# The Nyquist column of a folded DFT: from the matmul to a VectorE add at the eviction

## The chip, the cores and the metric

The kernel runs on one core of a Trainium2 chip. Time is the device time of one execution in microseconds; a kernel's time is the median over several executions. One execution is also recorded by the hardware profiler, and all durations of single instructions come from that one.

The engines are called PE (TensorE: matmul; PEld is its weight load), DVE (VectorE), ACT (ScalarE), POOL (GpSimd) and SP (SyncE, which only issues DMAs here).

## What is computed

The input x has 8 batches of 3008 tokens and 256 features (fp32). The reference, cut to what matters:

```
X = fft(x, axis=1); X = fft(X, axis=2); x = X.real        # over the tokens, then over the features
xt = x.transpose(0, 2, 1)
h  = max(xt @ w_tok1, 0) @ w_tok2                         # token mixing: 3008 -> 256 -> 3008
u  = x + h.transpose(0, 2, 1)
out = u + max(u @ w_ch1, 0) @ w_ch2                       # channel mixing: 256 -> 1536 -> 256
```

Only the real part is wanted, so the kernel uses the symmetry of the DFT: features d and 256 - d are added (even part) and subtracted (odd part) first, and cosines act on the even part and sines on the odd part. The even part has 129 values: d = 0, 1 to 127, and the Nyquist value d = 128, whose cosine over the output index is +1, -1, +1, and so on.

## The kernel before

All matmuls are in fp16 with sums in fp32. Every batch goes through two halves.

The *front* of a batch, `front(b)`, is a generator; each `yield` ends a step, and the main loop takes steps one by one.

- `fold` (GpSimd, for batch 0 VectorE) makes the even and odd parts `eo`: in its 256 features, columns 0 to 128 are the even part and 129 to 255 the odd part.
- 8 steps of the first token stage: matmuls of `eo` into PSUM tile pz, copied to `z`. The first half of `z` has features 0 to 127 of `eo`, the second half features 128 to 255; so partition 0 of the second half is the Nyquist value and partitions 1 to 127 are the odd part.
- 12 steps of the d stage, which the change touches (lines 439 to 446). Step g multiplies the two halves of z, as weights (128x128), by two tables: `td1` (259 columns) and `td0` (131 columns), both into PSUM tile pw. The result `w` has columns 0 to 130 for the cosine sums (column 1 and 130 are two half sums) and columns 132 to 258 for the sine sums. The odd part gives columns 132 to 258 only; of the 259 columns of `td1` the first 132 are zero except in row 0, which holds +0.5 and -0.5: there the Nyquist value is added to the cosine columns. `copy` (lines 287 to 291) evicts pw into w: with 0 on ScalarE, with 1 on VectorE. VectorE takes every second step of batch 0, and ScalarE all others.
- 2 steps with `pt` (line 455, 12 matmuls of 130 and 12 of 127 columns each), 3 steps with `pq` and `py` (line 482), and 12 steps with `pu` (line 506) finish the token mixing and give `ut`, the transposed u.

Every PSUM tile of the front comes from one pool with three buffers (tag "f": pz, pw, pt, px, py, pq, pu). `ps_mm` has three more for pc, and `ps_out` two for po.

The *channel half* of a batch works on 6 chunks of 512 tokens, each in 4 subtiles. In a subtile the program order is: `mm1`, three groups of two matmuls of 512 columns into pc (line 539), evicted with the max on ScalarE (line 542) twice and on VectorE (line 87 through `ts`) once; `mm2` for the chunk before, 12 matmuls of 256 columns into po (line 560), whose sums VectorE adds (line 574) in every second subtile; and then some steps of the next batch's front.

Nothing is reordered: each engine runs its instructions in program order, and the number of steps in every subtile is written out by hand:

```
plan = [[0] * 11 + [3, 3, 2, 4, 4, 4, 1, 1, 2, 1, 4, 4, 4],
        [2] * 4 + [2] * 6 + [1, 1] + [1] * 3 + [1, 2] * 4 + [0]]
```

The first list holds while batch 0 is in its channel half, the second after that. So the 12 d steps of batch 0 run alone, in setup; those of batch 1 run in three subtiles of batch 0, four in each (in the first and third behind a step of batch 0 with pu); and those of batches 2 to 7 run in six subtiles each, two in each, 72 steps in all.

Of the kernel before, what the change touches and what calls it, by code (L numbers as in the profile page):

```python
# [9 lines left out]
FP16 = mybir.dt.float16  # L10
FP32 = mybir.dt.float32
I32 = mybir.dt.int32
AT = mybir.AluOpType
# [6 lines left out]
P = 128  # L20
# [14 lines left out]
WD = 259  # L35
TWO23 = float(2.0 ** 23)
PI2 = float(2 * np.pi)
# [3 lines left out]
def kernel(  # L41
# [9 lines left out]
    nc = tc.nc  # L51
# [8 lines left out]
    const = ctx.enter_context(tc.tile_pool(name="const", bufs=1))  # L60
# [11 lines left out]
    def ps_f(name, dt=FP32, n=512):  # L72
        return psum.tile([P, n], dt, tag="f", name=name, bufs=3)
# [11 lines left out]
    def ts(out_, in_, s1, op0, s2=None, op1=None, eng=nc.vector):  # L85
        if op1 is None:
            eng.tensor_scalar(out=out_, in0=in_, scalar1=s1, scalar2=None, op0=op0)  # L87
        else:
            eng.tensor_scalar(out=out_, in0=in_, scalar1=s1, scalar2=s2,
                              op0=op0, op1=op1)  # L90
# [7 lines left out]
                                   in1=pcol[:], op0=AT.mult, op1=AT.add)  # L98
# [7 lines left out]
                                   op0=AT.mult, op1=AT.add)  # L106
# [53 lines left out]
    for t in (tp, tq):  # L160
        for i in range(2):
            h = slice(64 * i, 64 * i + 64)
            nc.scalar.activation(
                out=t[h, :, 64 - 64 * i:128 - 64 * i],
# [15 lines left out]
                                   op0=AT.mult, op1=AT.add)  # L180
# [6 lines left out]
                                   op0=AT.mult, op1=AT.add)  # L187
    nc.vector.scalar_tensor_tensor(out=reff[:], in0=eq32[:], scalar=1472.0, in1=reff[:],
                                   op0=AT.mult, op1=AT.add)
# [3 lines left out]
                                   op0=AT.mult, op1=AT.add)  # L193
    nc.vector.scalar_tensor_tensor(out=offq[:], in0=mid[:], scalar=-752.0, in1=tmp[:],
                                   op0=AT.mult, op1=AT.add)
# [27 lines left out]
    def reduced(m, period, nrow, width, eng=nc.vector):  # L223

        v = gen.tile([P, width], FP32, tag="gv", bufs=2, name="gv")[0:nrow, :]
        eng.tensor_scalar(out=v, in0=m, scalar1=1.0 / period, scalar2=TWO23,
                          op0=AT.mult, op1=AT.add)
        eng.tensor_scalar(out=v, in0=v, scalar1=-TWO23, scalar2=-float(period),
                          op0=AT.add, op1=AT.mult)
        r = gen.tile([P, width], FP32, tag="gr", bufs=2, name="gr")[0:nrow, :]  # L230
        eng.tensor_tensor(out=r, in0=v, in1=m, op=AT.add)
        return r

    def sin(out_, in_, scale):
        nc.scalar.activation(out=out_, in_=in_, func=AFT.Sin, scale=scale)
# [51 lines left out]
    def copy(e, out_, in_):  # L287
        if e:
            (nc.vector, nc.gpsimd)[e - 1].tensor_copy(out=out_, in_=in_)
        else:  # L290
            nc.scalar.activation(out=out_, in_=in_, func=AFT.Copy)  # L291
# [8 lines left out]
    pl = nc.gpsimd  # L300
# [28 lines left out]
    ts(md[:, 128:255], jrow[:, 1:128], pcol[:], AT.mult, eng=pl)  # L329
    rd = reduced(md[:], 256, P, 255, pl)  # L330
    td0 = const.tile([P, 131], FP16, tag="td0")
    td1 = const.tile([P, WD], FP16, tag="td1")
    sin(td0[:, 2:130], rd[:, 0:128], PI2 / 256)
    sin(td1[:, 132:WD], rd[:, 128:255], PI2 / 256)
    pl.memset(td0[:, 0:1], 1.0)
    ts(td0[:, 1:2], td0[:, 129:130], 0.5, AT.mult, 0.5, AT.add, eng=pl)
    ts(td0[:, 130:131], td0[:, 129:130], 0.5, AT.mult, -0.5, AT.add, eng=pl)
    ts(td0[0:1, :], td0[0:1, :], 0.5, AT.mult, eng=pl)
    pl.memset(td1[:, 0:132], 0.0)
    pl.memset(td1[0:1, 0:2], 0.5)  # L340
    pl.memset(td1[0:1, 3:130:2], 0.5)
    pl.memset(td1[0:1, 2:130:2], -0.5)


    tcol, sgn = pvec("tcol"), pvec("sgn")
# [29 lines left out]
    def w2_cols(b, c):  # L375
        return (w2p if b else w2v)[:, :, :, 8 * c:min(8 * c + 8, NQ)]
# [30 lines left out]
    def front(b):  # L407
# [3 lines left out]
        for t0 in (11, 6, 1):  # L411
            for half in range(2):
                c = slice(half * P, (half + 1) * P)
                pz = ps_f("pz")
                for k in range(5):
                    nc.tensor.matmul(pz[:, 96 * k:96 * k + 96], lhsT=eo[:, t0 + k, c],  # L416
                                     rhs=t1n[:].rearrange("p a b k -> p (a b k)"),
                                     start=True, stop=True)
# [4 lines left out]
        for half in range(2):  # L423
# [3 lines left out]
                             rhs=t1n[0:NQ, half, 0, :],  # L427
                             start=True, stop=True)
            if half:
                nc.tensor.matmul(pz[0:1, 0:24], lhsT=eo[0:NQ, 0, P:P + 1],  # L430
                                 rhs=t1n[0:NQ, 0, 0, :], start=True, stop=True)
            nc.tensor.matmul(pz[:, 24:96], lhsT=eo[:, 16, c],  # L432
                             rhs=t1b[:].rearrange("p a k -> p (a k)"),
                             start=True, stop=True)
# [3 lines left out]
        w = perb.tile([P, NG, WD], FP16, tag="w", name="w", bufs=2)  # L438
        for g in range(NG):
            pw = ps_f("pw")  # L440
            za = z[:, 0, 2 * g:2 * g + 2, :].rearrange("p a b -> p (a b)")
            zb = z[:, 1, 2 * g:2 * g + 2, :].rearrange("p a b -> p (a b)")
            nc.tensor.matmul(pw[:, 0:WD], lhsT=zb, rhs=td1[:], start=True, stop=False)  # L443
            nc.tensor.matmul(pw[:, 0:131], lhsT=za, rhs=td0[:], start=False, stop=True)  # L444
            copy(g % 2 and b == 0, w[:, g, :], pw[:, 0:WD])
            yield


# [1 line left out]
        for th in range(2):  # L450
            c = slice(th * P, (th + 1) * P)
            pt = ps_f("pt1")
            for o, n, f, hw in ((0, 130, 0, hp), (130, 127, 132, hq)):
                for g in range(NG):
                    nc.tensor.matmul(pt[:, o:o + n], lhsT=hw[:, g, c],  # L455
                                     rhs=w[:, g, f:f + n],
                                     start=(g == 0), stop=(g == NG - 1))
            if th == 0:
                px = ps_f("px")
                nc.tensor.matmul(px[:, 0:NG], lhsT=perm[:], rhs=w[:, :, 130],  # L460
                                 start=True, stop=True)
# [15 lines left out]
        for c in range(3):  # L477
            py, pq = ps_f("py"), ps_f("pq")
            for o, f, tab in ((pq, 131, tq), (py, 1, tp)):
                for k in range(4):  # L480
                    g = 4 * c + k
                    nc.tensor.matmul(o[:, P * k:P * k + P], lhsT=w[:, g, f:f + P],  # L482
                                     rhs=tab[:, g, :], start=True, stop=True)
            qs = perb.tile([P, CW], FP32, tag="qs", name="qs", bufs=2)
            nc.scalar.activation(out=qs[:], in_=pq[:], func=AFT.Copy)  # L485
            for h, op in ((0, AT.subtract), (1, AT.add)):
                nc.vector.tensor_tensor(out=yt[:, h, CW * c:CW * c + CW], in0=py[:],  # L487
                                        in1=qs[:], op=op)
# [10 lines left out]
        for c in range(NCH):  # L499
            f0 = CW * c  # L500
            n = min(CW, S - f0)
            for h in range(2):
                minus = c >= 3
                pu = ps_f("pu")
                for th in range(2):
                    nc.tensor.matmul(pu[:, 0:n], lhsT=uu[:, th, int(minus), h, :],  # L506
                                     rhs=w2_cols(b, c)[:, th],
                                     start=(th == 0), stop=(th == 1))
# [3 lines left out]
                else:  # L512
                    y = yt[:, h, f0:f0 + n]
                nc.vector.tensor_tensor(  # L514
                    out=ut[:, h, f0:f0 + n].rearrange("p (a b) -> p a b", b=64),
                    in0=pu[:, 0:n].rearrange("p (b a) -> p a b", b=64),
                    in1=y.rearrange("p (a b) -> p a b", b=64), op=AT.add)
# [85 lines left out]
    if BB > 1:  # L603
        x_tiles[1] = load_x(1)
    own = front(0)
    take(own, 4)
    carried(tts_p, hp)
# [16 lines left out]
    turned_u = {(0, 0): turn_u(0, 0)}  # L624
    for b in range(BB):
        nxt = front(b + 1) if b + 1 < BB else iter(())
        done, folded = 0, False
        for c in range(NCH):
# [60 lines left out]
```

## Time and profile before

| | |
|---|---|
| median of 9 runs | 644.05 us (642.79 to 644.88) |
| the profiled execution | 644.87 us, span 643.1 us |
| PE busy | 617.7 us (96%), 4778 matmuls |
| DVE, ACT, POOL busy | 331.3, 317.5, 251.1 us |
| granted TensorE clock, mean | 0.988 of full speed |
| line 443, pw, 128x259, 96 times | 274 ns each |
| line 444, pw, 128x131, 96 times | 221 ns each |
| line 291, ACT copy of pw to w, 90 times | 386 ns each |
| line 289, DVE copy of pw to w, 6 times | 426 ns each |

A line of the timeline or of the groups names the line of the program, the engine, the operation, the tiles (out<-in), their shapes and a count; a bracket holds how long the engine had been idle before and what ended that. A matmul's duration includes the time until its last result is out, and the next one starts long before that; the rate of matmuls is read from their starts. The chain of waits is followed back from the last instruction. In the table of stretches each row gives the stretch, its length, the busy time and count of PE, PEld, DVE, ACT and POOL, the granted clock, and the share of the DMA engines and their GB/s.

### The profile page before, as it was taken

What the parts mean: (1) busy time and instruction counts of PE and PEld (TensorE: products, weight loads), DVE (VectorE), ACT (ScalarE), POOL (GpSimd) and SP (SyncE); (2) the same over time, 40 slices, a digit from 0 to 9 for tenths busy, and PEclk for the clock granted to TensorE, in tenths of its full rate; (3) what the DMA queues carried; (4) which work ended last, traced back from release to release, by engine and by line L of the source; (5) the groups of instructions that cost most, each with busy time, mean ns of one, the idle gap of its engine ahead of it and who ended that gap; (6) DMA issues with size and microseconds to landing.
All of it is one profiled execution on the core that took longest, in us unless ns stands there. A gap on an engine that the chain in (4) does not pass through costs nothing.

```text
span 643.1 us, 11805 instructions
## 1 busy us (share of the span) xinstructions
PE 617.7 (96%) x4778; PEld 425.3 (66%) x4778; DVE 331.3 (52%) x702; ACT 317.5 (49%) x667; POOL 251.1 (39%) x250
## 2 busy tenths in 40 slices
PE   3789999999999999999999999999999999999996
PEld 3545667567766776667766676666766777666675
DVE  8755435733664437633565336643466336653442
ACT  7547465265535554365533655356533655334431
POOL 8819949669130880059411591039400000000000
PEclk9779999999999999999999999999999999999999
DMA  9992472732932268142763229223221521332332
GB/s 148 180 212 52 82 150 50 140 68 50 162 70 68 55 94 151 33 99 59 123 79 80 66 60 161 63 66 82 59 50 34 115 50 50 66 75 69 80 82 66
DMA packets 86550, 56.28 MB, mean 88 GB/s; under 512 B 54832, under 2 KB 83440, under 8 KB 85744
## 3 DMA queue, kind: packets, MB, share of 16 engines
q1 hardware_dynamic: 78240, 38.04, 27.7%
q0 software_dynamic: 8256, 17.49, 17.2%
q8 instruction: 37, 0.61, 0.4%
q14 instruction: 17, 0.14, 0.1%
HBM read 34.98 MB, written 24.64 MB: 93 GB/s over the span
## 4 chain that ended last, share of the span: by engine, by line
PE 93%; DMA 2%; DVE 2%; ACT 1%; POOL 1%; issue 1%; DVEq 0%; ACTq 0%; POOLq 0%
PE po L560 38%; PE pc L539 38%; PE pu L506 6%; PE pt L455 3%; DMA w1m<-in_moe_w_tok_dram 2%; PE pw L443 2%; PE pz L416 1%; PE pw L444 1%; PE py L482 1%; PE pq L482 1%; PE ph L365 1%; PE ph L363 1%; DVE yt L487 0%; DVE ut L514 0%; PE pz L432 0%
## 5 line engine op out<-in xcount | busy, mean ns | idle before, releaser
L542 ACT ACTIVATE c<-pc 128x512 f16<-128x512 f32 (+1 forms) x384 | 205.4, 588 | 171.8 <-PE pc L539 143.7
L560 PE MATMUL po<-wc,c 128*128 128x256 f16 x2256 | 276.4, 273 | 0.0
L560 PEld LDWEIGHTS <-c 128*128 128x128 f16 x2256 | 220.8, 98 | 63.1
L87 DVE TENSOR_SCALAR c<-pc 128x512 f16<-128x512 f32 (+1 forms) x192 | 130.5, 680 | 164.9 <-PE pc L539 145.9
L539 PE MATMUL pc<-ut,wc1p 128*128 128x512 f16 x576 | 141.3, 381 | 0.5 <-DVE ut L514 0.4
L539 PE MATMUL pc<-ut,wc1m 128*128 128x512 f16 (+1 forms) x576 | 134.9, 370 | 0.0
L574 DVE TENSOR_TENSOR osb<-po,rt 128x258 f32<-128x258 f32 (+3 forms) x240 | 74.7, 361 | 55.8 <-PE po L560 51.5
L539 PEld LDWEIGHTS <-wc1m 128*128 128x128 f16 x576 | 54.8, 98 | 54.0
L539 PEld LDWEIGHTS <-wc1p 128*128 128x128 f16 x576 | 53.1, 98 | 51.8 <-issue 5.6
L514 DVE TENSOR_TENSOR ut<-pu,yt 128x512 f16<-128x512 f32 (+1 forms) x96 | 61.6, 671 | 35.6 <-PE pu L506 35.6
L394 POOL TENSOR_TENSOR xd<-xp,xm 94x1024 f16<-94x1024 f16 x28 | 59.3, 2119 | 24.5 <-DVE c L87 13.8
L592 POOL COPY ch<-c 128x768 f16<-128x768 f16 x4 | 3.3, 824 | 155.6 <-DVE c L87 155.6
L395 POOL TENSOR_TENSOR xp<-xp,xm 94x1024 f16<-94x1024 f16 x28 | 59.4, 2120 | 2.2
L399 POOL TENSOR_TENSOR eo<-xp 94x512 f16<-94x512 f16 (+1 forms) x28 | 34.0, 1213 | 59.4 <-PE pz L432 58.2
L291 ACT ACTIVATE w<-pw 128x259 f16<-128x259 f32 x90 | 30.1, 386 | 49.6 <-PE pw L444 49.1
L594 POOL COPY c<-ch 128x768 f16<-128x768 f16 x4 | 3.3, 824 | 122.4 <-PE po L560 122.4
L291 ACT ACTIVATE z<-pz 128x480 f16<-128x480 f32 (+1 forms) x59 | 34.5, 674 | 24.4 <-PE pz L416 20.2
L506 PE MATMUL pu<-w2p,uu 128*128 128x512 f16 (+1 forms) x168 | 45.0, 379 | 1.2 <-DVE ut L514 1.2
L487 DVE TENSOR_TENSOR yt<-py,qs 128x512 f16<-128x512 f32 x48 | 30.7, 686 | 18.9 <-ACT qs L485 9.4
L403 POOL TENSOR_TENSOR eo<-xd 94x508 f16<-94x508 f16 (+1 forms) x28 | 33.7, 1204 | 0.0
L506 PEld LDWEIGHTS <-uu 128*128 128x128 f16 x192 | 19.0, 99 | 12.4 <-issue 3.4
L485 ACT ACTIVATE qs<-pq 128x512 f32<-128x512 f32 x24 | 14.1, 596 | 19.4 <-PE pq L482 9.2
(142 smaller groups left out, 378.8 us busy)
## 6 DMA issues: line engine op xcount, KB each, us to landing
out_dram<-osb SPq DMA_DIRECT2D x84, 256.0 KB, 3.4
xp<-in_x_dram POOLq DMA_DIRECT2D x16, 272.0 KB, 5.6
out_dram<-osb SPq DMA_DIRECT2D x12, 192.0 KB, 2.8
xp<-in_x_dram POOLq DMA_DIRECT2D x16, 127.5 KB, 5.9
rt<-ut SPq DMA_TRANSPOSE x96, 2.7
w2s<-in_moe_w_tok_dram POOLq DMA_DIRECT2D x1, 1504.0 KB, 19.0
w1p<-in_moe_w_tok_dram POOLq DMA_DIRECT2D x2, 384.0 KB, 10.3
wc<-in_moe_w_ch_dram POOLq DMA_DIRECT2D x1, 768.0 KB, 11.7
```

Source lines behind the costliest of these rows:

```text
L87: eng.tensor_scalar(out=out_, in0=in_, scalar1=s1, scalar2=None, op0=op0)
L291: nc.scalar.activation(out=out_, in_=in_, func=AFT.Copy)
L394: eng.tensor_tensor(out=xd[:, t, :], in0=xp[:, t, :], in1=rv, op=AT.subtract)
L395: eng.tensor_tensor(out=xp[:, t, :], in0=xp[:, t, :], in1=rv, op=AT.add)
L399: eng.tensor_tensor(out=eo[:, t, 1:129], in0=xp[:, t, 1:129], in1=xp[:, t, 255:127:-1], op=AT.add)
L403: eng.tensor_tensor(out=eo[:, t, 129:256], in0=xd[:, t, 1:128], in1=xd[:, t, 255:128:-1], op=AT.subtract)
L506: nc.tensor.matmul(pu[:, 0:n], lhsT=uu[:, th, int(minus), h, :], rhs=w2_cols(b, c)[:, th], start=(th == 0), stop=(th == 1))
L514: nc.vector.tensor_tensor(out=ut[:, h, f0:f0 + n].rearrange("p (a b) -> p a b", b=64), in0=pu[:, 0:n].rearrange("p (b a) -> p a b", b=64), ...
L539: nc.tensor.matmul(pc[:, 0:n], lhsT=wc[:, h, ct * P:(ct + 1) * P], rhs=ut[:, h, f0:f0 + n], start=(h == 0), stop=(h == 1))
L542: nc.scalar.activation(out=c1[:, ct, 0:n], in_=pc[:, 0:n], func=AFT.Relu)
L560: nc.tensor.matmul(po[0:n, o:o + D], lhsT=c1[:, ct, ks * P:ks * P + n], rhs=wc2[:, ct, :], start=(ct == 0), stop=(ct == NCT - 1))
L574: nc.vector.tensor_tensor(out=osb[r, ks_, j], in0=src[r, k0:k1, j], in1=rt[r, ks_, p], op=AT.add)
```

## The change

`td1` loses its first 131 columns: it has 128, of which the first is zero except for 0.5 in row 0, and its product with the second half of z is written to columns 131 to 258 of pw. Column 131 of pw then holds half of the Nyquist value, one number for each partition. The product with `td0` no longer adds onto it but is written to columns 0 to 130 by itself. At the eviction ScalarE copies the sine columns 132 to 258, in every step and batch, and VectorE writes columns 0 to 130 in one `scalar_tensor_tensor`: a new constant `alt` (+1, +1, -1, +1, ..., with 0 in the last column), times the number in column 131, plus the cosine columns. Column 131 of w is written later (from px), as before.

```diff
     td0 = const.tile([P, 131], FP16, tag="td0")
-    td1 = const.tile([P, WD], FP16, tag="td1")
+    td1 = const.tile([P, P], FP16, tag="td1")
+    alt = const.tile([P, 131], FP16, tag="alt")
     sin(td0[:, 2:130], rd[:, 0:128], PI2 / 256)
-    sin(td1[:, 132:WD], rd[:, 128:255], PI2 / 256)
+    sin(td1[:, 1:P], rd[:, 128:255], PI2 / 256)
...
-    pl.memset(td1[:, 0:132], 0.0)
-    pl.memset(td1[0:1, 0:2], 0.5)
-    pl.memset(td1[0:1, 3:130:2], 0.5)
-    pl.memset(td1[0:1, 2:130:2], -0.5)
+
+    pl.memset(td1[:, 0:1], 0.0)
+    pl.memset(td1[0:1, 0:1], 0.5)
+    pl.memset(alt[:], 1.0)
+    pl.memset(alt[:, 2:129:2], -1.0)
+    pl.memset(alt[:, 130:131], 0.0)
...
-            nc.tensor.matmul(pw[:, 0:WD], lhsT=zb, rhs=td1[:], start=True, stop=False)
-            nc.tensor.matmul(pw[:, 0:131], lhsT=za, rhs=td0[:], start=False, stop=True)
-            copy(g % 2 and b == 0, w[:, g, :], pw[:, 0:WD])
+            nc.tensor.matmul(pw[:, 131:WD], lhsT=zb, rhs=td1[:], start=True, stop=True)
+            nc.tensor.matmul(pw[:, 0:131], lhsT=za, rhs=td0[:], start=True, stop=True)
+            copy(0, w[:, g, 132:WD], pw[:, 132:WD])
+            nc.vector.scalar_tensor_tensor(
+                out=w[:, g, 0:131], in0=alt[:], scalar=pw[:, 131:132],
+                in1=pw[:, 0:131], op0=AT.mult, op1=AT.add)
             yield
```

In the changed kernel the two matmuls stand on lines 446 and 447 and the VectorE operation on line 449; later lines are shifted by six. Its line 291 is the ScalarE copy still.

## The prediction

> **What bounds the kernel now.** I read the page's busy times first, then the chain of work that ended last.
>
> ```profile
> PE 617.7 (96%) x4778; PEld 425.3 (66%) x4778; DVE 331.3 (52%) x702; ACT 317.5 (49%) x667; POOL 251.1 (39%) x250
> PE 93%; DMA 2%; DVE 2%; ACT 1%; POOL 1%; issue 1%; DVEq 0%; ACTq 0%; POOLq 0%
> ```
>
> TensorE is on 93% of the chain, so a moving column that is removed is worth its full time wherever TensorE runs without gaps. Whether it does where the changed lines stand, the timeline tells. There are three kinds of places: 12 of the 96 steps of the d stage belong to batch 0 and run alone in setup, 12 belong to batch 1 and run four at a time, and 72 (batches 2 to 7) run two at a time between the channel matmuls. First a pair of the 72:
>
> ```profile
> 141.44 0.27 PE L443 MATMUL pw<-td,z 128*128 128x259 f16 x1
> 141.55 0.22 PE L444 MATMUL pw<-td,z 128*128 128x131 f16 x1
> 141.60 0.27 PE L443 MATMUL pw<-td,z 128*128 128x259 f16 x1
> 141.64 0.76 DVE L574 TENSOR_TENSOR osb<-po,rt 128x258 f32<-128x258 f32 x2 [0.62 <-PE po L560]
> 141.72 0.22 PE L444 MATMUL pw<-td,z 128*128 128x131 f16 x1
> 141.77 1.46 PE L539 MATMUL pc<-ut,wc1p 128*128 128x512 f16 x6
> 141.81 0.66 ACT L291 ACTIVATE w<-pw 128x259 f16<-128x259 f32 x2 [1.26 <-PE pw L444]
> 143.27 0.69 DVE L87 TENSOR_SCALAR c<-pc 128x512 f16<-128x512 f32 x1 [0.88 <-PE pc L539]
> ```
>
> Starts, not durations, give the rate: 259 columns take 0.11 us, 131 take 0.055, a step takes 0.166, and the pc matmuls follow with no gap. The evictions lie beside them, and VectorE has 0.88 us idle before its next pc eviction. Between 138.39 and 153.00 us the stretch view gives PE 14.61 us busy of 14.61.
>
> In setup it is different:
>
> ```profile
> 31.45 0.69 DVE L289 CAST hq<-ph 128x512 f16<-128x512 f32 x1 [0.25 <-PE ph L365]
> 31.61 0.73 ACT L291 ACTIVATE w<-pw 128x259 f16<-128x259 f32 x2
> 32.06 1.30 DVE L289 CAST w<-pw 128x259 f16<-128x259 f32 x3
> ```
>
> The 12 steps of batch 0 run from 31.25 to 34.56, 0.276 us each although TensorE needs 0.166: they are paced by evictions into three PSUM buffers, with ScalarE and VectorE taking turns. Columns saved there are worth nothing by themselves.
>
> The last view is the waits:
>
> ```profile
> DVE uv L466 <- ACT sq L464: 24.9, 16, 2.5
> ```
>
> L466 reads only pt, not sq, and yet it waited 16 times of 16 for ScalarE's copy out of the same PSUM tile. Two engines that read one PSUM tile are put one after the other in this program. The changed eviction reads pw with both engines, and the instruction order of the changed kernel (which can be read before it runs) shows the same: each new VectorE operation waits for ScalarE's copy of its tile, and each later pw matmul that needs a buffer waits for VectorE. So the two halves of the eviction are a chain, not parallel.
>
> **TensorE, 72 steps.** 390 columns become 128 + 131 = 259. The nearest row for two such matmuls with alternating weights is the token stage, 130 and 127 columns, all 128x128 weights:
>
> ```profile
> 98.31 1.36 PE pt L455 x24
> ```
>
> 1.36 / 24 = 0.0567 us each, so a new step takes at most 0.113; scaling 0.166 by 259/390 gives 0.110. I take 0.112, a saving of 0.054 a step, 72 x 0.054 = 3.9 us (3.8 to 4.0). One thing has no row: the first matmul's output now begins at an odd PSUM column (131). Bounds: nothing, or at worst its 0.055 becomes 0.11, which takes the whole saving. I take nothing, as the token stage writes from mid-bank (column 130) and L443 and L444 have odd widths, all at the normal rate. No gain is possible beyond the columns.
>
> The Trainium skill speaks against this ("TensorE: Matmul & The Clock Gate", Back-to-back issue gap): it gives about 81 ns a matmul at 128 columns once weight loads are counted. By it, an estimate, a new step would take 0.162 us, 72 steps would save 0.3 us, and the whole sum would come to +0.7. The 0.0567 us above, with a weight load before every matmul, differs, and the measurement decides.
>
> **Eviction, the durations.** ScalarE's 128x259 copy (386 ns) becomes 128x127; the row is L464, 128x127 out of PSUM, 0.27 us, the next one about 0.20 later. VectorE gets 96 operations of 131 elements with one PSUM and one SBUF input; the row is L467, 128x127, 280 ns, with its successor starting 0.20 later (36.66, 36.86). Upper bound: two cycles for an element or a slow scalar, twice the 0.14 us by which 128x254 (416 ns) exceeds that row, so 0.42 us with a spacing of 0.34. It can't be under the 0.16 of the smallest rows. I take 0.28. VectorE rises by 96 x 0.28 - 6 x 0.43 = 24 us, ScalarE falls by 90 x 0.386 - 96 x 0.27 = 9 us.
>
> **Is that hidden in the 72 steps?** Behind the new operation in VectorE's queue is the pc eviction L87, for which the PSUM buffer of pc and then the po matmuls wait. In the pair above: osb ends at 142.40, the two new operations start at 142.32 and 142.52 (ScalarE is done by then) and end at 142.80, L87 is due at 143.27 less 0.11 of saved TensorE time, 143.16. A margin of 0.36; with the 0.42 us operation 0.08. Every second subtile has no osb and more room. Cost nothing; without that cover a pair would cost up to 0.5 us. The next pair's buffers are due at 144.2, 1.4 us after. The longest wait of osb for rt (0.6 us) fits too.
>
> **Batch 0, 12 steps.** VectorE starts at 32.06 as now, after hq. Then a buffer's round is: second matmul starts 0.055 after the first, result 0.22, to ScalarE 0.04, copy 0.27, to VectorE 0.03, operation 0.28, to TensorE 0.05: 0.945 us for three steps, 0.315 a step instead of 0.276. Rounds start on TensorE at 32.39, 33.34, 34.28; the last operation runs from 35.30 to 35.58, and the twelfth hp matmul, which reads it, starts at 35.63 instead of 34.56 + 11 x 0.057 = 35.19. Cost 0.44 us; with 0.42 us operations 1.3; if steps overlap better than this, 0.
>
> **Batch 1, 12 steps, four at a time.** The fourth step waits for the first one's buffer. In the first group VectorE is busy with ut until 87.49, its first new operation runs 87.41 to 87.69, the fourth step starts at 87.74 and pc at 87.85 (now 87.74): +0.11. In the second, osb holds VectorE until 91.31; the operation runs 91.25 to 91.53, the fourth step starts at 91.58, pc at 91.69 (now 91.32): +0.37. The third is like the first: +0.07. Sum +0.55, against 1.0 with the slow operation. So the 24 early steps lose 1.0 us together.
>
> **The rest.** GpSimd's four memsets of td1 (0.5 us at 24.3) become five of td1 and alt; what follows in its queue (perm at 25.94, the wc1 loads at 26.7) moves by 0.2 us at most, and perm is needed at 35.9, wc1 at 44.45. Sine widths are unchanged. Nothing.
>
> **Sum.** -3.9 + 0.44 + 0.55 = -2.9 us. The profiled execution took 644.87 us (span 643.1), at the top of the nine runs (642.79 to 644.88, median 644.05); the difference carries over to the median: 641.1 us, profiled about 642.0.
>
> **Rivals.**
> The clock falls. The granted clock halved at 40.4 us after a stretch of one 3.4 us grid step (steps of 3.41 fit the changes at 26.75, 40.37 and 47.15):
>
> ```profile
> 30.16:33.58 3.42, 3.26 (x29) 2.48 (x28) 2.70 (x7) 2.53 (x6) 2.81 (x6) 1.00 0.89 118
> 36.99:40.37 3.38, 1.58 (x25) 1.28 (x23) 0.97 (x5) 2.58 (x9) 0.00 (x0) 1.00 1.31 265
> 40.37:43.80 3.43, 2.97 (x15) 1.37 (x13) 3.43 (x8) 0.78 (x2) 0.00 (x0) 0.50 1.01 199
> ```
>
> A step with PE busy 47% led to half clock; after the change the step 30.16 to 33.58 has about 2.5 us busy of 3.42, 73%, where now it has 95%. No row says what 73% does. If the clock falls at 33.58, the token stage runs at half rate: +1.7 to 2.2 us, net -1.2 to -0.7, 642.9 to 643.4. The skill's same page (Part 1: The HAM clock gate) asks for at least one idle window of about 3.4 us before the clock drops. By it no drop comes here, and yet none would explain 40.4 either, where PE was 47% busy. Chance 0.08.
>
> The short matmul isn't short (the slower side). Each weight load of z lasts 98 ns. If L446 and L447 can't overlap theirs, a step takes 0.196 instead of 0.166: 72 x 0.03 = +2.2, with the early 1.0 +3.2 us, 647.3. It decides from 83 ns a matmul up. Against it stands 0.0567. The odd column at its worst belongs here too: no saving, +1.0 us, 645.0. Chance 0.07 together, most of it for the weight loads and their like.
>
> The hand-off is dearer: 0.42 us operations give -3.9 + 1.3 + 1.0 = -1.6, 642.4; still faster, part of the forecast's range. That the change doesn't do what it says is excluded by the instruction order: 96 VectorE operations, matmuls of 128 and 131 columns.
>
> **Numbers.** The forecast has 0.85, the clock 0.08, the long matmul 0.07. The range goes from -4.0 + 0.3 less 0.4 for the spread of medians, 639.9, to the far end of the clock case, 643.3. About 0.2% (1.3 us) is what can be told from no change, so faster means under 642.76: the forecast but for its upper tail, 0.83; the clock case and that tail are the same, 0.11; slower 0.06.
>
> **What would show it.** Right: L446 and L447 start 0.055 apart in the paired steps, the subtile of 2.94 us becomes 2.83, L449 waits for ScalarE and no pc matmul waits for VectorE there, and batch 0's d stage ends 0.4 us later. Wrong: starts over 0.08 apart, L449 over 0.4 us, TensorE waiting in the paired steps, or half clock between 33 and 37 us.

## The result and the profile after

The changed kernel took 641.32 us (median of 11 runs, 640.47 to 642.42), the kernel before 643.95 (33 runs): 2.6 us less by the medians. The ratio of the runs is 0.9963 with a 95% interval of 0.9953 to 0.9973, which is 1.7 to 3.0 us less. That is inside the range and 0.2 us from the forecast; the chance of 0.83 stood on this side. A second measurement, on another occasion, gave 642.26 against 644.31, ratio 0.9970 (0.9959 to 0.9981). Medians here and below are of fast runs; one run of late_only (898 us) and one of before_actcopy (1311 us) are slow and left out.

The page after, busy times and chain:

```profile
PE 612.3 (96%) x4778; PEld 422.2 (66%) x4778; DVE 355.9 (56%) x792; ACT 311.2 (49%) x673; POOL 251.2 (39%) x251
PE 90%; DVE 1%; ACT 1%; issue 0%; DVEq 0%; ACTq 0%
```

TensorE is still the bound, with 5.4 us less busy time; VectorE has 24.6 us more (24 were worked out), and ScalarE 6.3 less (9 were worked out). The pair of d steps in the timeline that answers to the one at 141.44 us:

```profile
141.71 0.22 PE L446 MATMUL pw<-td,z 128*128 128x128 f16 x1
141.77 0.22 PE L447 MATMUL pw<-td,z 128*128 128x131 f16 x1
141.83 0.22 PE L446 MATMUL pw<-td,z 128*128 128x128 f16 x1
141.88 0.22 PE L447 MATMUL pw<-td,z 128*128 128x131 f16 x1
141.91 0.76 DVE L580 TENSOR_TENSOR osb<-po,rt 128x258 f32<-128x258 f32 x2 [0.62 <-PE po L566]
141.94 1.46 PE L545 MATMUL pc<-ut,wc1p 128*128 128x512 f16 x6
142.03 0.44 ACT L291 ACTIVATE w<-pw 128x127 f16<-128x127 f32 x2 [1.20 <-PE pw L447]
142.59 0.62 DVE L449 SCALAR_TENSOR_TENSOR w<-alt,pw 128x131 f16<-128x131 f16 x2
143.44 0.69 DVE L87 TENSOR_SCALAR c<-pc 128x512 f16<-128x512 f32 x1 [0.24 <-PE pc L545]
```

Starts are 0.05 to 0.06 us apart, pc follows without a gap 0.23 us after the first start (it was 0.33), and VectorE still has 0.24 us idle ahead of its pc eviction, where it had 0.88. That the output of L446 begins at an odd PSUM column costs nothing. The setup:

```profile
30.39 0.69 DVE L289 CAST hq<-ph 128x512 f16<-128x512 f32 x1 [0.25 <-PE ph L368]
31.00 3.98 DVE L449 SCALAR_TENSOR_TENSOR w<-alt,pw 128x131 f16<-128x131 f16 x12
31.39 0.22 PE L446 MATMUL pw<-td,z 128*128 128x128 f16 x1 [0.70 <-DVE w L449]
34.49 1.42 PE L461 MATMUL pt<-w,hp 128*128 128x130 f16 x12 [0.22 <-DVE w L449]
```

Now TensorE waits for VectorE: the fourth step at 31.39, and the first pt matmul at 34.49. And the waits show the hand-off from ScalarE that was read off L466 (total us, times, longest us):

```profile
DVE w L449 <- ACT w L291: 18.2, 19, 1.0
```

The two spans differ by 3.6 us (643.1 and 639.5), more than the medians. To sort this, I compare starts of the same matmuls in the profiles, stretch by stretch. "d stage" is from the first pw to the first pt matmul of batch 0; "groups" is the sum over the three groups of batch 1, from the first pw to the pc behind them; "batches 2 to 7" is from the first paired step to the pc behind the last one; "px to po" is the rest of the setup of batch 0, up to the first po.

| profile of | d stage | groups | batches 2 to 7 | px to po |
|---|---|---|---|---|
| before | 3.31 | 3.26 | 387.77 | 17.77 |
| after | 4.31 | 3.96 | 383.87 | 17.07 |
| early_only | 4.31 | 3.96 | 387.75 | 18.45 |
| evict_only | 4.47 | 4.13 | 387.75 | 18.60 |
| matmul_only | 3.33 | 2.91 | 383.87 | 16.90 |
| imm_scalar | 4.04 | 3.76 | 383.87 | 16.91 |
| late_tables | 3.31 | 3.25 | 383.86 | 17.77 |
| late_both | 3.31 | 3.25 | 383.86 | 17.04 |

The first three columns repeat to 0.02 us between kernels with the same form at that place; the last does not, and it goes with the clock (below). The change is -3.90 + 1.00 + 0.70 = -2.2 us in the first three columns. The rest of the 3.6 us lies in three other places, beside px to po. The first pw starts at 31.25 us before and at 30.18 after; in before_actcopy, whose code up to there is that of before, it starts at 30.17, so this is no effect of the change (half clock ended at 26.7, 24.3 and 24.4 us in the three). From the first pt to px the changed kernel needs 2.49 us instead of 1.36, at half clock. And the pu steps of batch 1 differ by 0.7 us, which is the matter of a copy (below).

### The profile page after: what moved, and what is told of

Same layout as the page of the kernel before. It is cut to its first block, busy times and chain, and to the rows that moved or that the text cites. A ratio compares the mean times of both kernels' runs of the same rounds, so it can differ in the third digit from the quotient of the medians.

```text
span 639.5 us, 11902 instructions
## 1 busy us (share of the span) xinstructions
PE 612.3 (96%) x4778; PEld 422.2 (66%) x4778; DVE 355.9 (56%) x792; ACT 311.2 (49%) x673; POOL 251.2 (39%) x251
## 4 chain that ended last, share of the span: by engine, by line
PE 90%; DVE 1%; ACT 1%; issue 0%; DVEq 0%; ACTq 0%
PE po L566 39%; PE pc L545 37%; PE pu L512 6%; PE pt L461 3%; PE pz L419 1%; PE pw L446 1%; PE py L488 1%; PE pq L488 1%; PE pw L447 1%; DVE ut L520 1%; ACT c L548 1%; DVE osb L580 0%; ACT w2p L291 0%; PE pz L435 0%; PE pz L429 0%
## 5 line engine op out<-in xcount | busy, mean ns | idle before, releaser
L291 ACT ACTIVATE z<-pz 128x480 f16<-128x480 f32 (+1 forms) x59 | 34.4, 672 | 24.3 <-PE pz L419 20.1
L291 ACT ACTIVATE w<-pw 128x127 f16<-128x127 f32 x96 | 21.9, 276 | 48.9 <-PE pw L447 48.9
L449 DVE SCALAR_TENSOR_TENSOR w<-alt,pw 128x131 f16<-128x131 f16 x96 | 29.5, 352 | 18.9 <-ACT w L291 18.2
```

## The experiments

### The new form in some of the batches

`late_only` uses it in batches 2 to 7, `early_only` in batches 0 and 1. Both keep the old table td1 and make tn1 and alt right behind it; in the new branch stands the changed kernel's step, with tn1 for td1.

```diff
+            if b >= 2:                      # early_only: b < 2
...
+            else:
                 nc.tensor.matmul(pw[:, 0:WD], lhsT=zb, rhs=td1[:], start=True, stop=False)
                 nc.tensor.matmul(pw[:, 0:131], lhsT=za, rhs=td0[:], start=False, stop=True)
                 copy(g % 2 and b == 0, w[:, g, :], pw[:, 0:WD])
```

Expected of late_only:

> The new form for batches 2 to 7 only; batches 0 and 1 keep the long matmuls and the old copies. Theory (all of the gain is TensorE time in the 72 paired steps, 0.054 us each, and the 24 early steps only lose): 72 x 0.054 = 3.9 us less than before, 640.0 us, ratio 0.994; the early part of the profile lies as before. Rival (the early steps cost nothing in the median, and the 72 steps yield just the 2.6 us that were measured): the same as the changed kernel, 641.3 us, ratio 0.996.

Expected of early_only:

> The new form for batches 0 and 1 only. Theory: slower than before by what the 24 early steps lose, 3.9 - 2.6 = 1.3 us by the medians (0.7 of it in batch 1, as the profile after shows), 645.2 us, ratio 1.002. Rival (they cost nothing, the difference between early parts of the two profiles is the clock and chance): 643.9 us, ratio 1.000.

late_only: 641.35 us, ratio 0.9966 (0.9951 to 0.9982). early_only: 646.64 us, ratio 1.0046 (1.0031 to 1.0062). early_only's interval lies clear on the slow side, as the theory has it, and by the profiles the 72 steps save 3.9 us in late_only (383.86 us for batches 2 to 7) and nothing in early_only. But both medians lie about 1.4 us above the theory's numbers, and late_only's falls on the number of its rival (641.3). What the two share is GpSimd work for the second table ahead of the loads of the channel weights (0.9 us in late_only's profile); late_tables moves it away. Whether that is the cause is taken up there.

### The two halves of the change, each alone

`evict_only` keeps the new eviction and gives the matmul its 259 columns back; `matmul_only` has the short matmuls and the old copies, and leaves the Nyquist term out of the cosine sums.

```diff
 # evict_only, against the changed kernel
-    td1 = const.tile([P, P], FP16, tag="td1")
+    td1 = const.tile([P, WD], FP16, tag="td1")
...
-    pl.memset(td1[:, 0:1], 0.0)
-    pl.memset(td1[0:1, 0:1], 0.5)
+    pl.memset(td1[:, 0:132], 0.0)
+    pl.memset(td1[0:1, 131:132], 0.5)
...
-            nc.tensor.matmul(pw[:, 131:WD], lhsT=zb, rhs=td1[:], start=True, stop=True)
-            nc.tensor.matmul(pw[:, 0:131], lhsT=za, rhs=td0[:], start=True, stop=True)
+            nc.tensor.matmul(pw[:, 0:WD], lhsT=zb, rhs=td1[:], start=True, stop=False)
+            nc.tensor.matmul(pw[:, 0:131], lhsT=za, rhs=td0[:], start=False, stop=True)
 # matmul_only, against the changed kernel
-            copy(0, w[:, g, 132:WD], pw[:, 132:WD])
-            nc.vector.scalar_tensor_tensor(...)
+            copy(g % 2 and b == 0, w[:, g, :], pw[:, 0:WD])
```

Expected of evict_only:

> The new eviction on two engines for all batches, but the matmuls have 259 and 131 columns again (the first 131 columns of the table are zeros), so TensorE saves nothing. Theory (the eviction is hidden in the paired steps and costs only in the early ones): +0.7 in batch 1 and about 0.6 to 1.0 in batch 0, so 1.3 to 1.7 us, 645.5 us, ratio 1.0024; in a paired step pc follows without a gap. Rival (VectorE's 25 us more also hold up something in the paired steps, 0.02 us a step or more): 1.4 us on top, 647 us, ratio 1.005.

Expected of matmul_only:

> The short matmuls for all batches with the old eviction (one copy of 259 columns; the Nyquist term is left out of the cosine sums). Theory (columns are worth their time only where TensorE runs without gaps): 3.9 us in the paired steps, 0.1 to 0.3 in batch 1, next to nothing in batch 0, where evictions set the pace: 639.8 us, ratio 0.9935. Rival (every column counts): 96 x 0.054 = 5.2 us, 638.8 us, ratio 0.992.

evict_only: 646.59 us, ratio 1.0047 (1.0029 to 1.0064). matmul_only: 640.26 us, ratio 0.9949 (0.9931 to 0.9966). A pair of evict_only in the timeline:

```profile
142.54 0.27 PE L446 MATMUL pw<-td,z 128*128 128x259 f16 x1
142.65 0.22 PE L447 MATMUL pw<-td,z 128*128 128x131 f16 x1
...
142.88 1.46 PE L545 MATMUL pc<-ut,wc1p 128*128 128x512 f16 x6
...
144.37 0.69 DVE L87 TENSOR_SCALAR c<-pc 128x512 f16<-128x512 f32 x1 [0.34 <-PE pc L545]
```

pc comes 0.34 us after the first start, as before, and the stretch of batches 2 to 7 is 387.75 us. So in this profile VectorE's 25 us more are hidden in the paired steps entirely, and what the rival said of them is out. The median, though, fell on the rival's number (647 us, 1.005) and not on the theory's 645.5; the early stretches lose 1.16 and 0.87, 2.0 us, and the other 1.0 us is not explained. matmul_only's profile shows that columns saved in the d stage of batch 0 are worth nothing (3.33 against 3.31 us), in batch 1 0.35 us, and in the paired steps 3.90. Its median is 3.4 us under before, where these add up to 4.2. It can't be added up with evict_only: in the early stages the eviction sets the pace, and in the paired steps TensorE.

### The new form in batches 2 to 7, tables made later

`late_tables` is late_only with the six GpSimd instructions for tn1 and alt, a copy and five memsets, moved behind the fold of batch 1. The changed kernel ran once more beside it.

```diff
         x_tiles[2] = load_x(2)
+    pl.tensor_copy(out=tn1[:, 1:P], in_=td1[:, 132:WD])
...
     setup.close()
```

Expected of late_tables:

> The new form for batches 2 to 7 only, as in the run late_only, but GpSimd makes the two extra tables after the fold of batch 1 and not ahead of the loads of the channel weights. Theory (nothing is lost early): 3.9 us under before, about 640.0 us, and 1.7 under the changed kernel. Rival (the early steps cost nothing in the median, as late_only's 2.2 us would have it): no better than the changed kernel beside it.

Expected of the changed kernel, again:

> The changed kernel once more, beside the next two. Theory (3.9 us saved in the paired steps, 1.0 lost in batch 0 and 0.7 in batch 1): 2.2 us under before, 641.5 us; in its profile the d stage of batch 0 takes 4.3 us to the first pt matmul (3.3 before) and the three groups of batch 1 lose 0.7. The half clock that the first profile showed between 34.6 and 38.0 us need not come again, since the grid of clock steps lies elsewhere in each execution.

late_tables: 641.11 us against 644.31, ratio 0.9948 (0.9934 to 0.9961); the changed kernel: 642.26, ratio 0.9970 (0.9959 to 0.9981). -3.9 us is 0.9939, inside the first interval; -2.2 is 0.9966, inside the second. The early steps cost 1.15 us by these medians, whose intervals just touch, and 1.7 by the profiles.

That GpSimd's work ahead of the loads made late_only slower is not shown. The intervals of late_only and late_tables overlap, and late_only's own profile has no such loss: its first pw starts at 31.57 us, where late_tables has 31.24, and its run took 640.15 us. Nor does the second table fit the other runs of that measurement: against the kernel before beside them (643.61), late_only, early_only, evict_only and matmul_only all lie 0.9 to 1.6 us above what the stretches of their profiles add up to, and the last two have no second table. They were compared with the same 13 runs of the kernel before; what lifted all four stays open.

The profile of the changed kernel's second measurement has the d stage at 4.31 us and full clock through it and the token stage (the first pt to px 1.36 us, 2.49 in the first profile).

### What makes the VectorE operation long

The row of two tensors (L467) had 280 ns; L449 took 351. `imm_scalar` has scalar=0.5, `sbuf_scalar` a constant column in SBUF; both leave the Nyquist value out of the sum.

```diff
-                out=w[:, g, 0:131], in0=alt[:], scalar=pw[:, 131:132],
+                out=w[:, g, 0:131], in0=alt[:], scalar=0.5,           # sbuf_scalar: scalar=mask0[:]
```

Expected of imm_scalar:

> The VectorE operation takes the constant 0.5 in place of the number in column 131, so the Nyquist term of the cosine sums is wrong. Theory A (the pointer to a number is what makes the operation 351 ns instead of the 280 of the row of two tensors): 280 ns. Theory B (the operation of three inputs itself is longer): 350 ns.

Expected of sbuf_scalar:

> The changed kernel, but the VectorE operation takes its number for each partition from a constant in SBUF and not from column 131 in PSUM, so the Nyquist term is wrong. Theory A1 (a pointer as such costs the 66 ns that the constant saved): 350 ns. Theory A2 (it is the reading of the number from PSUM): 285 ns.

The line of the operation in the changed kernel, then in imm_scalar, then in sbuf_scalar (min, median, max in ns):

```profile
L449 DVE SCALAR_TENSOR_TENSOR w<-alt,pw x96: 347/351/360, 31.0 to 523.7; 128x131 f16<-128x131 f16 x96
```

```profile
L449 DVE SCALAR_TENSOR_TENSOR w<-alt,pw x96: 282/285/296, 32.1 to 523.0; 128x131 f16<-128x131 f16 x96
```

```profile
L449 DVE SCALAR_TENSOR_TENSOR w<-alt,mask,pw x96: 342/346/355, 31.2 to 524.2; 128x131 f16<-128x131 f16 x96
```

285 ns with a constant: the third operand is free, and so theory B falls. A pointer (a number for each partition, read from memory) costs 61 ns from SBUF and 66 from PSUM: it is the pointer as such (A1). In imm_scalar the d stage takes 4.04 us instead of 4.31 and the groups 3.76 instead of 3.96: so much of the early loss is the pointer. (640.67 and 641.9 us in one run each are not used.)

### Keeping TensorE busy in the d stage of batch 0

```diff
+            if b == 0:
+                filler(3)                   # three 128-column matmuls whose result nobody reads
```

> The changed kernel with three 128-column matmuls without use behind each of the 12 d steps of batch 0, which fill TensorE's waits there. Theory of the clock (the thin stage can end in half clock): full clock in the profile from 30 us to the end of the token stage, and the median 0.3 to 1 us under the changed kernel's beside it, the slowest runs most. Rival (the clock falls there too seldom to matter): the same median within 0.3 us. If the fillers hold up the stage itself, its 4.3 us become longer.

642.40 us, ratio 0.9974 (0.9961 to 0.9986), beside 642.26 for the changed kernel: no gain. In the profile the clock stayed full to the end of the token stage, but the d stage took 5.14 us instead of 4.31. The first three rounds start as in the changed kernel (31.38, 32.41, 33.45); in the last one ScalarE's first copy starts only at 34.42 (33.77 in the changed kernel), and why is not shown. The median is the one that the rival named, but a loss of 0.8 us in the stage itself can hide a gain of that size, so this run does not decide between the two.

### Fillers at another place, and one copy moved

`late_filled` is late_tables with fillers behind the pt steps (12 each) and the first two yt steps (8 each) of batch 0; `late_both` also moves VectorE's copy of the last columns of ut to ScalarE, and `before_actcopy` does only that to the kernel before.

```diff
+            if b == 0:
+                filler(12)                  # behind the pt step; filler(8) behind yt steps 0 and 1
...
-            nc.vector.tensor_copy(out=ut[:, :, S:NCH * CW],
-                                  in_=state[b - 1]["ut"][:, :, S - 64:S])
+            nc.scalar.activation(out=ut[:, :, S:NCH * CW],
+                                 in_=state[b - 1]["ut"][:, :, S - 64:S], func=AFT.Copy)
```

Expected of late_filled:

> As late_tables (new form for batches 2 to 7 only), and in the setup of batch 0 TensorE gets matmuls without use (12 behind each pt step, 8 behind the first two yt steps) where it waits for the other engines. Theory of the clock (most executions run part of the stretch from 40 to 47 us at half clock because TensorE is thin there; without that, from px to the first po matmul takes 16.9 us, as in the profile of matmul_only, and not the 17.8 of before): full clock there and 0.5 to 1 us less than late_tables, ratio 0.9935. Rival (the fillers lie in the way, or the stretch is set by VectorE and ScalarE): the same ratio as late_tables, 0.995.

Expected of late_both:

> As late_filled, and the copy of 2x64 columns of ut from the batch before (for odd batches) goes to ScalarE instead of VectorE. Theory (VectorE's SBUF to SBUF copy, 0.18 us by itself, stands still while a GpSimd operation of the fold runs, 0.4 to 1.35 us in the profiles, and the pu step behind it waits): 0.4 us under late_filled. Rival (ScalarE's copy is itself later): no gain.

Expected of before_actcopy:

> The kernel before with only that copy moved to ScalarE. Theory: the pu stretch of batch 1 (113.20 to 116.09 us, 2.9 us, in the profile of before; 2.2 in the changed kernel's, where the copy met no fold) takes 2.2 us, and the median falls by 0.4 to 0.7 us: ratio 0.999. Rival (the 0.7 us between the two first profiles there came from the change): the stretch keeps its 2.9 us.

| | median | before | ratio | interval |
|---|---|---|---|---|
| late_filled | 639.96 | 643.81 | 0.9940 | 0.9926 to 0.9955 |
| late_both | 639.36 | 643.81 | 0.9926 | 0.9911 to 0.9940 |
| before_actcopy | 643.93 | 643.81 | 0.9998 | 0.9987 to 1.0009 |

late_both beats both kernels: 4.5 us under before, and its interval lies clear of the changed kernel's 0.9963 and 0.9970. From late_tables to late_filled the profile has what the theory says (full clock, px to po 17.04 us and not 17.77), but one profile each does not show that the fillers did it: matmul_only and imm_scalar had full clock there without them. The intervals overlap too, so the 0.5 us in the table is not shown by the medians.

The copy: in before_actcopy the stretch of the pu steps of batch 1 takes 2.10 us and not 2.89. In the profiles of late_filled and late_both the starts agree to 0.15 us from the d stage of batch 0 up to these pu steps, and behind the copy late_both is 2.0 us ahead (the copy took 1.93 us in late_filled). So the copy holds up TensorE by an amount that differs between executions, and the 0.7 us between the first two profiles there was not the change's: the second profile of the changed kernel has 2.78 us for this stretch. The medians show less. late_both lies 0.6 us under late_filled with overlapping intervals, and the kernel before gains nothing measurable; its interval excludes a gain of more than 0.8 us.

## Why the prediction was right, point by point

**The 72 paired steps: right.** 0.054 us a step and 3.9 us were predicted; 3.90 us is what every profile with short matmuls in batches 2 to 7 shows (383.86 or 383.87 against 387.77), and none with long ones. The row that carried it was the token stage's 0.0567 us a matmul. The 81 ns of the Trainium skill ("TensorE: Matmul & The Clock Gate", Back-to-back issue gap) do not hold here, and with them the long matmul, the slower rival, is out: starts are 0.05 to 0.06 us apart with a weight load for each.

**Hidden in the paired steps: right,** with less room than worked out. The margin ahead of the pc eviction was put at 0.36 us; it is 0.24, because the operation took 0.35 us.

**The hand-off: right in kind, cheap by a quarter in size.** The wait of VectorE for ScalarE and of TensorE for VectorE came where they were put. The duration did not: 0.28 was taken from a row without a pointer, with 0.42 as the upper bound, and 0.351 was measured, with a spacing of 0.27 instead of 0.20. A round of three steps took 1.03 us (31.39, 32.42, 33.46) instead of 0.945.

**Batch 0: the mis-sized term.** 0.44 us was predicted and 1.00 measured. Of the difference 0.27 is the pointer (4.31 to 4.04 in imm_scalar). With the duration that had been assumed, the rounds of imm_scalar come as worked out: 0.96 to 0.97 us each, where 0.945 was predicted. What is left there, 0.73 instead of 0.44, is mostly a wait that the working left out: it let pt start as soon as TensorE was free and wait only at the twelfth matmul, but the first pt matmul already waits for a late operation. In the changed kernel VectorE's tenth starts at 34.08, so it ends at 34.43, and pt starts at 34.49; the first pt matmul has a wait, the next nine have none, and the last two have one again. So the matmuls of pt read w piece by piece, but they wait for it in larger pieces. In imm_scalar the last operation ends at 35.69 and the twelfth pt matmul starts at 35.96, though by that operation alone it could have started about 0.2 us earlier. In the changed kernel's second profile, at full clock, the same two are 35.29 and 35.43: there the wait alone is worth about 0.1 us, and the longer chain makes up the rest.

**Batch 1: right, a little cheap.** +0.11, +0.37 and +0.07 were predicted; +0.18, +0.41 and +0.11 measured, 0.70 instead of 0.55. With the constant in place of the pointer it is 0.50.

**The sum.** -2.9 us was predicted. The repeatable stretches give -2.2, so the early steps were 0.7 us too cheap; the two measurements give -2.6 and -2.05 by the medians, and the interval of the second (-1.2 to -2.6 us) leaves out -2.9. That the forecast of 641.1 came so near 641.3 is in part luck with the setup: -2.2 alone would be 641.75.

**The rival of the clock: it occurred, and did not decide.** Half clock between 33 and 37 us had been named as a sign of being wrong, and it came in the first profile. Two rows of the stretch view of the changed kernel:

```profile
31.16:34.57 3.41, 2.51 (x20) 1.45 (x20) 2.99 (x11) 2.42 (x9) 2.56 (x4) 1.00 0.89 141
34.57:37.98 3.41, 3.41 (x34) 3.41 (x34) 0.75 (x5) 0.36 (x3) 0.28 (x1) 0.50 1.37 191
```

The d stage had PE busy 74% of a grid step (73% was predicted), and the next step ran at half clock. It cost 1.13 us up to px and 0.43 in the second half of the token stage, 1.6 together, where 1.7 to 2.2 had been priced. But the profile of before had a half clock from 40 to 47 us that this one did not, so from px to po the changed kernel was 0.7 us faster. In the second profile of the changed kernel the clock fell elsewhere (42.4 us). Where it falls differs between executions, of both kernels; with it the start of the first pw lies between 30.2 and 31.6 us in the profiles, and px to po takes 16.7 to 18.7.

## What to carry to other kernels

Price a matmul by the spacing of starts in the stage where it stands: the same 131 columns were worth 0.054 us a step between dense matmuls, about half of that in groups of four, and nothing where evictions set the pace. An eviction that two engines share on one PSUM tile was a chain here, so use it where its latency is covered (late_tables: 72 of 96 steps, 1.7 us better than the changed kernel by the profiles) and keep the one-engine copy where it is not. Where profiles of two kernels differ by more than the medians, compare the starts of the same matmuls stretch by stretch before a cause is named.

## What the runs showed of the hardware

**A pointer scalar costs VectorE 61 to 66 ns an operation** in this `scalar_tensor_tensor` of 131 elements, from SBUF as from PSUM; a third operand as a constant costs nothing over two tensors (285 against 280 ns, for 4 more elements).

**An fp16 VectorE copy from SBUF to SBUF stands still while GpSimd works.** The copy of 128x128 takes 0.18 us alone (changed kernel). In late_tables it met the fold:

```profile
114.05 1.38 POOL L401 TENSOR_TENSOR eo<-xp 94x640 f16<-94x640 f16 x1
114.13 1.35 DVE L504 COPY ut<-ut 128x128 f16<-128x128 f16 x1
...
116.13 0.59 PE L516 MATMUL pu<-w2p,uu 128*128 128x512 f16 x2 [1.48 <-DVE ut L524]
```

It ends at 115.48, 0.05 after GpSimd's operation, and TensorE waits 1.48 us for what VectorE does behind it. The Trainium skill ("SBUF — State Buffer", Who interferes with whom) says that VectorE's two-port modes and GpSimd lock each other out for a whole instruction; this agrees, though the trace does not tell which mode the copy ran in. The same copy took 0.87 us in the profile of before, 0.18 and 0.77 in the two profiles of the changed kernel, and 1.93 in late_filled's. Each time but the 0.18 it ended 0.05 or 0.06 us after a GpSimd operation. Its time depends on how the two meet in an execution, and this makes 0.7 us of the 3.6 between the first two spans.

**The clock's steps in setup.** The changes of the granted clock lie on a grid of 3.41 us whose place differs between executions (a change at 40.3 in before and late_tables, 42.4 in the second run of the changed kernel, none between 27 and 638 us in imm_scalar). The time of before goes with it, loosely: in the runs beside the experiments those at a mean granted clock of 0.997 took 642.2 to 642.4 us and those at 0.987 or 0.988 took 644.2 to 645.4, but one at 0.996 took 644.3 and one at 0.999 took 643.0. What makes it fall stays open: after a step with PE 74% busy it fell at 34.57, and after this row of the same profile, with 58%, it did not.

```profile
37.98:41.39 3.41, 1.97 (x31) 1.68 (x30) 0.89 (x6) 2.54 (x9) 0.00 (x0) 1.00 1.20 280
```

**Not settled:** early_only and evict_only are 3.0 us slower than before by the medians, with intervals from 2.0 to 4.0 and 1.9 to 4.1, where the repeatable stretches give 1.7 and 2.0. Their profiles have half clock for two grid steps from 42 us (px to po 18.45 and 18.60), but that of before_actcopy has it too (18.74), and its median is close to before's (643.93 and 643.81). late_only and matmul_only of the same measurement lie above their stretches as well, by 1.6 and 0.9 us.
